# Layer one's last pair in seven partial second products, and block 2's low parts written in layer two

## The chip, the cores and the metric

One core of one Trainium2 chip runs the whole program. The metric is the device time of one execution in microseconds (us). Its engines are TensorE (PE in the rows; PEld is its weight loads), VectorE (DVE), ScalarE (ACT), GpSimd (POOL) and SyncE (SP), which issues the transfers. Each works through its own instructions in order and waits on semaphores of the others.

## The reference

Attention with cluster masks feeds two feed-forward layers, one after the other:

```
x = attention(q, k, v, centroids)             # 1536 tokens x 512, all float32
x = g1(x @ moe_w_in) @ moe_w_out              # 512 -> 2048 -> 512, g1(h) = max(0.01 h, h)
y = g2(x @ moe2_w_in) @ moe2_w_out            # 512 -> 2048 -> 512, g2(h) = relu(h) * relu(h)
```

## The kernel before, in words

The change lies in the two layers, so only these are told. Activations lie in SBUF transposed: features on the 128 partitions, tokens along the free axis. The 1536 tokens are three blocks of 512 (block 0, 1, 2), and the 512 features are four groups `o` of 128.

**Split products.** A float32 operand is kept as two parts in the format that TensorE multiplies: a high part (`xh`, `wh`, `gh`, `th`), which is the rounded value and is written by ScalarE, and a low part (`xl`, `wl`, `gl`, `tl`), which is the value minus its high part and is written by VectorE or GpSimd. A product is three matmuls: high by high, and each high by the other's low.

**Pairs.** A layer's 2048 inner features are 16 groups `f` of 128, worked on two at a time: a pair. First products make `h` (input weights by `x`) in the four banks U, V, W, X (`bank(i)`, tile `h`). Activations make `gh` and `gl`. Second products multiply these by the output weights into banks `o0` to `o3`, and `flush` adds them to the sums `acc` in SBUF, one 128x512 tile for each block and group.

**Seven for eight.** A pair with its two blocks 0 and 1 is a 2x2 product. In `quad` the first products are done with seven partial products in place of eight, on sums of weights (blocks with j = 2, made on GpSimd) and on sums of `x` (`th`, `tl`, made by `t_ops`). In `seven`, for the pairs listed in `SEVEN`, the second products are too: M1 to M7 on sums of the output weights (j = 3) and on sums of activations (T1 to T4). `rN.j` flushes partial product N. Block 2 is done plainly (`u0`, `u1`, then `o0` to `o3` with `f0` to `f3`).

**What sets the order.** In the layers the order on every engine but SP is the program's: the strings `SEVEN_QUAD` and the like are lists of steps that are issued one after the other, and the lists in `step_list` are interleaved with tables (`TURN`, `TURN_LAST`, `TURN_SEAM`, `SUMS`) that say after which step a piece of the coming weights or of the `x` sums is issued. The pieces of a weight block are: 0 load, 1 magnitude on ScalarE and `low` on GpSimd (L200), 2 join on VectorE (L206), 3 high part on ScalarE (L167), 4 low part on GpSimd (L168). One buffer `wraw` holds a load, so the next load starts when the join before it is done.

**The seam.** Pair 14 is layer one's last. There `flush` makes the new `x`: it adds, ScalarE writes `xh` and then `xl` is written, by GpSimd for blocks 0 and 1. For block 2 the sum stays in the bank (`o`), and VectorE subtracts from there, all four groups at the end. Pair 14 uses `quad` and plain second products (48 matmuls for blocks 0 and 1, `g2`). Layer two's first pair is plain: its steps are unit (0,0), unit (0,1), unit (1,0), out (0,0), unit (1,1), out (0,1), unit (2,0) and so on, 12 matmuls each, where unit (b,j) reads `xh` and `xl` of block b, all four groups in turn.

Of the kernel before, what the change touches and what calls it, by code (L numbers as in the profile page):

```python
# [80 lines left out]
def attention_moe_moe_kernel(  # L81
# [26 lines left out]
    SEVEN = (4, 6, 8, 10, 12)  # L108
# [53 lines left out]
    def split_block(ci, t):  # L162
        pool = next(q for q, n in ring if ci % RING < n)
        wh = pool.tile([128, 2 * DM], F32R, tag="wh", name="wh")
        wl = pool.tile([128, 2 * DM], F32R, tag="wl", name="wl")
        weights[blocks[ci]] = (wh, wl)
        nc.scalar.copy(out=wh, in_=t)  # L167
        return lambda: nc.gpsimd.tensor_tensor(  # L168
            out=wl, in0=t, in1=wh.bitcast(F32), op=ALU.subtract
        )  # L170

    def decode_pieces(ci):
# [41 lines left out]
        def rest():  # L214
            st["rest"]()
# [11 lines left out]
    def sum_pieces(ci):  # L227

        st = {}
        K = DM // 2  # L230

        def sums():
            w = st["w"] = stg[1].tile([128, 4, K], F32, tag="ws", name="ws")
            m, f, j = blocks[ci]
            t0, t1 = (words[blocks.index((m, f, i))] for i in range(2))
            if j == 2:
                a11, a12, a21, a22 = t0[:, 0:K], t0[:, K : 2 * K], t1[:, 0:K], t1[:, K : 2 * K]
            else:
                a11, a12, a21, a22 = (
                    t[:, DM + i * K : DM + (i + 1) * K] for i in range(2) for t in (t0, t1)  # L240
                )
            for o, i, k, op in (
                (w[:, 0], a21, a22, ALU.add),
                (w[:, 1], w[:, 0], a11, ALU.subtract),
                (w[:, 2], a11, a21, ALU.subtract),
                (w[:, 3], a12, w[:, 1], ALU.subtract),
            ):
                nc.gpsimd.tensor_tensor(out=o, in0=i, in1=k, op=op)

        def high():  # L250
            st["rest"] = split_block(ci, st["w"].rearrange("p a b -> p (a b)"))

        return [sums, high, lambda: st["rest"]()]
# [772 lines left out]
    x_low = []  # L1026

    def flush(m, b, g, o, ps, part=slice(0, 512)):
# [30 lines left out]
    def quad(m, f, behind=True):  # L1059
# [11 lines left out]
        def first():  # L1071
            p(U, lambda k: w_in(f0, k), lambda k: x_in(k, 0), True)
            p1 = tmp()
            nc.scalar.copy(out=p1, in_=U)
            p(V, lambda k: w_in(f0, 2 + k), lambda k: x_in(2 + k, 0), True)
            add(V, V, p1)
            if behind:
                act(m, 0, f, V)
# [3 lines left out]
        def second():  # L1082
# [4 lines left out]
            if not behind:  # L1087
                act(m, 0, f, V)
# [30 lines left out]
    def seven(f, prev, after, later):  # L1119
# [119 lines left out]
        for name, q, block, c, g, b, half in (  # L1239
# [8 lines left out]
            for j in range(2):  # L1248
                ops[f"r{name}.{j}"] = lambda q=q, j=j, b=b, o=2 * half + j: flush(
                    0, b, f // 2, o, st[q, j]  # L1250
# [8 lines left out]
        for o in range(4):  # L1259
            ops[f"o{o}"] = lambda o=o: last(o)  # L1260
            ops[f"f{o}"] = lambda o=o: flush(0, 2, f // 2, o, st["o", o])
        for i, q in enumerate(prev):
            ops[f"bh{i}"] = lambda q=q: g2(*q)
        for c, base in (("n", after), ("l", later), ("c", (0, f))):
            for k in range(4):
                for j in range(5):
                    ops[f"{c}{k}.{j}"] = lambda base=base, k=k, j=j: piece((*base, k), j)
        for kk in range(2):
            ops[f"h4.{kk}"] = t_by[0][kk]["h4"]
        for name in (SEVEN_PLAIN if f < 2 * PLAIN[0] else SEVEN_QUAD).split():  # L1270
# [66 lines left out]
    def step_list(m, f, prev):  # L1337
# [18 lines left out]
        first, second, third = quad(m, f, bool(behind))  # L1356
        behind = behind or [lambda: None] * 2
# [14 lines left out]
    TURN_LAST = TURN[:9] + (  # L1372
        TURN[9] + ((3, 1),), ((3, 2),), ((4, 0),), (),
    )
    TURN_SEAM = (
        (), ((0, 3),), ((1, 1),), ((0, 4), (1, 2)), (), ((2, 0), (3, 0)),
# [10 lines left out]
            -2: "t1.0 t1.1 t2.0 t2.1", -1: "t4.0 t4.1", 0: "t3.0 t3.1", 2: "h1.0 h1.1 l1.0 l1.1",  # L1387
# [6 lines left out]
    def piece(block, j):  # L1394
# [5 lines left out]
        pieces[block][j]()  # L1400
# [12 lines left out]
    for m in range(2):  # L1413
        turn = 0
        for f in range(0, NF, 2):
# [18 lines left out]
            for i, step in enumerate(seq):  # L1434
# [5 lines left out]
                table = {(0, NF - 2): TURN_LAST, (1, 0): TURN_SEAM}.get((m, f), TURN)  # L1440
# [5 lines left out]
                if m == 0 and f == NF - 2:  # L1446
                    sums(1, i - len(seq))
# [48 lines left out]
```

## Time and profile before

| | |
|---|---|
| time, median of 3 runs | 744.39 us (744.38 to 744.74) |
| the profiled execution's own time | 744.36 us |
| its span, first to last instruction | 742.6 us |
| TensorE busy | 735.8 us, 99% |
| VectorE, ScalarE, GpSimd busy | 533.1, 453.4, 494.1 us |
| layer one's pairs 6 to 12 | 30.00 us each |
| pair 14, then layer two | from 455.82 us, from 487.67 us |

Busy time is a union over an engine's instructions, and TensorE's overlap: a 512-column matmul lasts 0.39 us, and the next starts 0.23 us after it. The chain of waits counts each instruction from where the one before it ended. Lines L1 to L1495 are those of the kernel before.

### The profile page before, as it was taken

The page shows a single profiled execution, that of the slowest core. Times are in us where ns is not written, and L with a number is a line of the kernel's source. Part 1 is how long each engine was busy: PE and PEld are TensorE (multiplying, and loading weights), DVE is VectorE, ACT ScalarE, POOL GpSimd, SP SyncE. Part 2 cuts the span into 40 slices and gives each one's busy share as a digit, 9 for nine tenths or more (in the row PEclk, how much of TensorE's full clock was granted, in tenths as well). Part 3 has the DMA queues.
Part 4 walks back from the last instruction along what each step waited for, and adds up shares of the span by engine and source line. Part 5 has one row for each costly group of instructions (what it writes and reads, how often), then busy time and mean ns, then how long its engine had stood idle before and what let it go on. Part 6 is the DMA issues. An engine that isn't in the chain of part 4 may idle for free.

```text
span 742.6 us, 11189 instructions
## 1 busy us (share of the span) xinstructions
PE 735.8 (99%) x4018; PEld 641.2 (86%) x4018; DVE 533.1 (72%) x844; ACT 453.4 (61%) x837; POOL 494.1 (67%) x465
## 2 busy tenths in 40 slices
PE   9999999999999999999999999999999999999998
PEld 8999999999998878888888888888888888888886
DVE  7999999999997535477676866564666666676655
ACT  7988988988997564456365373656634335443430
POOL 7999999999957738686787883699434343343400
PEclk9999999999999999999999999999999999999999
DMA  5694574572603311112121131111312112121004
GB/s 148 167 222 113 117 181 109 107 189 67 164 1 116 113 57 57 56 57 99 59 71 56 57 114 47 67 58 56 101 42 85 57 57 77 45 106 58 1 0 170
DMA packets 16727, 65.52 MB, mean 88 GB/s; under 512 B 3120, under 2 KB 4272, under 8 KB 11680
## 3 DMA queue, kind: packets, MB, share of 16 engines
q1 hardware_dynamic: 16672, 64.81, 29.7%
q8 instruction: 32, 0.52, 0.3%
q14 instruction: 23, 0.19, 0.1%
HBM read 43.02 MB, written 3.15 MB: 62 GB/s over the span
## 4 chain that ended last, share of the span: by engine, by line
PE 93%; ACT 3%; DVE 2%; POOL 1%; issue 1%; POOLq 0%; ACTq 0%; DVEq 0%
PE h L914 32%; PE o L992 23%; PE A L578 8%; PE S L481 7%; PE T L543 7%; PE o L1221 6%; PE h L1221 4%; PE S L351 1%; ACT e L513 1%; DVE nm L503 1%; PE warm L291 1%; PE o L1022 1%; DVE el L560 1%; ACT eh L554 0%; PE dots L351 0%
## 5 line engine op out<-in xcount | busy, mean ns | idle before, releaser
L168 POOL TENSOR_TENSOR wl<-wt,wh 128x1024 fp32r<-128x1024 f32 x32 | 77.4, 2420 | 74.4 <-ACT wh L167 73.9
L914 PE MATMUL h<-xh,wh 128*128 128x512 f32 x288 | 112.1, 391 | 0.3 <-DVE h L1067 0.3
L914 PE MATMUL h<-xh,wl 128*128 128x512 f32 x288 | 112.2, 390 | 0.0
L914 PE MATMUL h<-xl,wh 128*128 128x512 f32 x288 | 112.1, 389 | 0.0
L1034 DVE TENSOR_TENSOR acc<-o,acc 128x512 f32<-128x512 f32 x154 | 100.0, 686 | 11.8 <-PE o L992 11.8
L560 DVE TENSOR_TENSOR el<-T,eh 128x512 fp32r<-128x512 f32 x144 | 94.6, 683 | 2.8 <-ACT eh L554 2.0
L530 POOL TENSOR_SCALAR e<-e,r 128x768 f32<-128x768 f32 x96 | 86.8, 917 | 12.5 <-PE T L543 6.7
L503 DVE TENSOR_REDUCE nm<-S 128x1 f32<-128x768 f32 x96 | 90.9, 949 | 3.6 <-PE S L351 1.9
L513 ACT ACTIVATE e<-S,nm 128x768 f32<-128x768 f32 x96 | 87.2, 909 | 9.9 <-DVE ds L379 5.4
L481 PE MATMUL S<-hb 128*128 128x384 f32 (+1 forms) x384 | 89.4, 347 | 0.4 <-ACT xt L591 0.3
L554 ACT CAST eh<-T 128x512 fp32r<-128x512 f32 x144 | 79.7, 590 | 8.8 <-PE T L543 8.6
L963 DVE TENSOR_TENSOR gl<-h,gh 128x512 fp32r<-128x512 f32 x66 | 45.0, 691 | 54.0 <-ACT h L958 35.5
L578 PE MATMUL A<-eh,vv 128*128 128x256 f32 x288 | 80.3, 308 | 0.6 <-DVE xt L600 0.6
L543 PE MATMUL T<-ident,e 128*128 128x128 f32 x576 | 79.7, 273 | 0.5 <-POOL e L530 0.5
L578 PE MATMUL A<-el,vv 128*128 128x256 f32 x288 | 73.0, 283 | 0.2 <-DVE el L560 0.2
L543 PEld LDWEIGHTS T<-ident,e 128*128 128x128 f32 x576 | 68.9, 143 | 3.6 <-POOL e L530 0.7
L992 PE MATMUL o<-wh,gh 128*128 128x512 f32 x184 | 71.6, 389 | 0.0
L992 PE MATMUL o<-wl,gh 128*128 128x512 f32 x184 | 71.6, 389 | 0.0
L992 PE MATMUL o<-wh,gl 128*128 128x512 f32 x184 | 71.6, 389 | 0.0
L948 ACT ACTIVATE t<-h 128x512 f32<-128x512 f32 x48 | 28.0, 599 | 71.3 <-PE h L914 38.0
L168 POOL TENSOR_TENSOR wl<-ws,wh 128x1024 fp32r<-128x1024 f32 x17 | 41.4, 2434 | 38.3 <-ACT wh L167 38.3
L914 PEld LDWEIGHTS h<-xh,wh 128*128 128x128 f32 x288 | 54.1, 188 | 12.5 <-DVE gl L1181 0.8
(187 smaller groups left out, 1739.9 us busy)
## 6 DMA issues: line engine op xcount, KB each, us to landing
wraw<-w SPq DMA_DIRECT2D x32, 1024.0 KB, 4.7
hb<-spl SPq DMA_DIRECT2D x14, 576.0 KB, 4.7
hb<-spl SPq DMA_DIRECT2D x42, 192.0 KB, 5.1
rqk<-qk SPq DMA_DIRECT2D x16, 384.0 KB, 4.0
rv<-v SPq DMA_DIRECT2D x8, 384.0 KB, 3.5
out<-q SPq DMA_DIRECT2D x11, 256.0 KB, 2.0
hb<-st SPq DMA_DIRECT2D x56, 24.0 KB, 2.1
hb<-hb SPq DMA_DIRECT2D x5, 144.0 KB, 8.2
```

Of the source, the lines that this page charges most:

```text
L168: return lambda: nc.gpsimd.tensor_tensor(out=wl, in0=t, in1=wh.bitcast(F32), op=ALU.subtract)
L481: nc.tensor.matmul(out=s[:, c, 0:HALF], lhsT=hb[0:k, a, i * 128 : (i + 1) * 128], rhs=hb[0:k, b, c * HALF : (c + 1) * HALF], start=(a == 0 ...
L503: nc.vector.tensor_reduce(out=n, in_=s_t[t][:, :, 0:HALF], axis=AX.XY, op=ALU.max, negate=True)
L513: nc.scalar.activation(out=e.rearrange("p (a b) -> p a b", a=2), in_=s_t.pop(t)[:, :, 0:HALF], func=AF.Exp, bias=n_t.pop(t), scale=1.0, ac ...
L530: nc.gpsimd.tensor_scalar(out=e_t[t], in0=e_t[t], scalar1=r_t[t // 2][:, t % 2 : t % 2 + 1], scalar2=1.0, op0=ALU.mult, op1=ALU.mult,)
L543: nc.tensor.transpose(T[:, o : o + 128], e_t[2 * u + b][:, kc * 128 : (kc + 1) * 128], ident)
L554: nc.scalar.copy(out=eh[:, 2 * g : 2 * g + 2, :].rearrange("p a b -> p (a b)"), in_=T_t[u, g])
L560: nc.vector.tensor_tensor(out=el[:, 2 * g : 2 * g + 2, :].rearrange("p a b -> p (a b)"), in0=T_t.pop((u, g)), in1=eh[:, 2 * g : 2 * g + 2, ...
L578: nc.tensor.matmul(out=A, lhsT=w, rhs=m[:, kc, :], start=(kc == 0 and i == 0), stop=(kc == KC - 1 and i == 1),)
L914: nc.tensor.matmul(out=out, lhsT=l, rhs=r, start=(first and i == 0), stop=(i == n - 1), skip_group_check=not first,)
L992: nc.tensor.matmul(out=outs[o], lhsT=l, rhs=r, start=(first and i == 0), stop=(last and i == 2),)
L1034: nc.vector.tensor_tensor(out=a, in0=ps, in1=a, op=ALU.add)
```

## The change

Pair 14 joins `SEVEN`, with an order of its own, `SEVEN_LAST`. Its first 54 products are in the order of the other pairs; the second products are M1 to M7 (42 matmuls) for blocks 0 and 1. A fourth weight block, (0, 14, 3), is made for it. The sum for `x` now ends in `acc` for every block, also for block 2, and its low part reads `acc` and `xh`, both in SBUF. For blocks 0 and 1 GpSimd writes it as before, but for block 0's groups 2 and 3 VectorE does (`x0.2`, `x0.3`), and for block 2 VectorE does so in layer two, two groups after step 3 and two after step 4 of its first pair. The `x` sums t1, t2 and t4 move into `SEVEN_LAST`, and of weight block (1, 2, 0) the join and of (1, 2, 1) the load move from pair 14 to step 0 of layer two.

```diff
+SEVEN_LAST = SEVEN_FIRST + (
+    "M1 M2 r1.0 r1.1 r2.0 r2.1 B22l l0.0 u1 u1h u1f u1l M6 M5 r6.0 r5.0 r5.1 r6.1 o0 f0 M3 T4h r3.0 M7 "
+    "r7.0 T4l r7.1 r3.1 o1 f1 M4 r4.0 r4.1 x0.2 x0.3 l0.1 t1.0 t1.1 t2.0 t2.1 t4.0 t4.1 o2 f2 o3 f3"
+)
...
-    SEVEN = (4, 6, 8, 10, 12)
+    SEVEN = (4, 6, 8, 10, 12, 14)
...
-    def flush(m, b, g, o, ps, part=slice(0, 512)):
+    def flush(m, b, g, o, ps, part=slice(0, 512), later=None):
...
-            x, eng = (ps, nc.vector) if b == 2 else (a, nc.gpsimd)
-            nc.vector.tensor_tensor(out=x, in0=ps, in1=a, op=ALU.add)
-            nc.scalar.copy(out=xh[:, o, c], in_=x)
-            if b == 2:
-                x_low.append((o, c, x))
-                if o < 3:
-                    return
...
+            nc.vector.tensor_tensor(out=a, in0=ps, in1=a, op=ALU.add)
+            nc.scalar.copy(out=xh[:, o, c], in_=a)
+
+            def low(eng):
+                eng.tensor_tensor(
+                    out=xl[:, o, c], in0=a, in1=xh[:, o, c].bitcast(F32), op=ALU.subtract
+                )
+
+            if later is not None:
+                later[b, o] = low
             else:
...
+                low(nc.gpsimd)
...
+            ops[f"f{o}"] = lambda o=o: flush(0, 2, f // 2, o, st["o", o], later=x_low)
+            ops[f"x0.{o}"] = lambda o=o: x_low[0, o](nc.vector)
...
-            return seq + [lambda: g2(*tail[0]), lambda: g2(*tail[1])], []
...
     TURN_SEAM = (
-        (), ((0, 3),), ((1, 1),), ((0, 4), (1, 2)), (), ((2, 0), (3, 0)),
+        ((0, 2), (1, 0)), ((0, 3),), (), ((1, 1), (0, 4)), ((1, 2),), ((2, 0), (3, 0)),
...
-            -2: "t1.0 t1.1 t2.0 t2.1", -1: "t4.0 t4.1", 0: "t3.0 t3.1", 2: "h1.0 h1.1 l1.0 l1.1",
+            0: "t3.0 t3.1", 2: "h1.0 h1.1 l1.0 l1.1",
...
+                if (m, f) == (1, 0) and i in (3, 4):
+                    for o in (2 * i - 6, 2 * i - 5):
+                        x_low[2, o](nc.vector)
```

VectorE, at the seam, before: the first three rows close layer one (the third is block 2's low parts, read from the banks `o`), the others are the activations of layer two's first units and the join of `wt`.

```order
L206 SCALAR_TENSOR_TENSOR wt<-wt,wraw 128x1024
L1039 TENSOR_TENSOR o<-o,acc 128x512 x4
L1050 TENSOR_TENSOR xl<-o,xh 128x512 x4
L951 SCALAR_TENSOR_TENSOR h<-h,t 128x512
L963 TENSOR_TENSOR gl<-h,gh 128x512
L951 SCALAR_TENSOR_TENSOR h<-h,t 128x512
L963 TENSOR_TENSOR gl<-h,gh 128x512
L951 SCALAR_TENSOR_TENSOR h<-h,t 128x512
L963 TENSOR_TENSOR gl<-h,gh 128x512
L206 SCALAR_TENSOR_TENSOR wt<-wt,wraw 128x1024
```

VectorE, the same place, after, from the low parts of block 0's groups 2 and 3 to the last two of block 2.

```order
L1045 TENSOR_TENSOR xl<-acc,xh 128x512 x2
L1041 TENSOR_TENSOR acc<-h,acc 128x512 x2
L956 SCALAR_TENSOR_TENSOR h<-h,t 128x512
L968 TENSOR_TENSOR gl<-h,gh 128x512
L211 SCALAR_TENSOR_TENSOR wt<-wt,wraw 128x1024
...
L968 TENSOR_TENSOR gl<-h,gh 128x512
L1045 TENSOR_TENSOR xl<-acc,xh 128x512 x2
L956 SCALAR_TENSOR_TENSOR h<-h,t 128x512
L968 TENSOR_TENSOR gl<-h,gh 128x512
L211 SCALAR_TENSOR_TENSOR wt<-wt,wraw 128x1024
L1045 TENSOR_TENSOR xl<-acc,xh 128x512 x2
```

The four low parts of block 2 stand in two twos now, the second behind the activations of unit (1,1) and behind the join of weight block (1, 2, 1).

GpSimd at the seam, before: low parts of `x` (L1050), sums of `x` (L1289) and their low parts (L1295), and weights (L200 and L168).

```order
L1050 TENSOR_TENSOR xl<-acc,xh 128x512 x4
L168 TENSOR_TENSOR wl<-wt,wh 128x1024
L200 TENSOR_SCALAR wraw<-wraw 128x1024
L1050 TENSOR_TENSOR xl<-acc,xh 128x512 x4
L1289 TENSOR_TENSOR q<-acc 128x512 x2
L1289 TENSOR_TENSOR q<-acc,q 128x512 x2
L1289 TENSOR_TENSOR t_5861<-acc,q 128x512
L1289 TENSOR_TENSOR t_5863<-acc,q 128x512
L1289 TENSOR_TENSOR q<-acc 128x512 x2
L200 TENSOR_SCALAR wraw<-wraw 128x1024
L1295 TENSOR_TENSOR tl<-q,th 128x512 x2
L168 TENSOR_TENSOR wl<-wt,wh 128x1024
```

GpSimd, the same place, after.

```order
L173 TENSOR_TENSOR wl<-wt,wh 128x1024
L1045 TENSOR_TENSOR xl<-acc,xh 128x512 x6
L205 TENSOR_SCALAR wraw<-wraw 128x1024
L1297 TENSOR_TENSOR q<-acc 128x512 x2
L1297 TENSOR_TENSOR q<-acc,q 128x512 x2
L1297 TENSOR_TENSOR t_5862<-acc,q 128x512
L1297 TENSOR_TENSOR t_5864<-acc,q 128x512
L1297 TENSOR_TENSOR q<-acc 128x512 x2
L1303 TENSOR_TENSOR tl<-q,th 128x512 x2
L205 TENSOR_SCALAR wraw<-wraw 128x1024
L173 TENSOR_TENSOR wl<-wt,wh 128x1024
L1303 TENSOR_TENSOR tl<-q,th 128x512 x2
```

Two low parts of `x` fewer, and the second `wraw` step (L205), for which VectorE's second join waits, stands behind two `tl` instead of ahead of them; a `wl` of 1024 columns follows it at once.

## Rows read from the trace of the kernel before

**Rows 1.** The page: each engine's busy time, then the granted clock by slice.

```profile
PE 735.8 (99%) x4018; PEld 641.2 (86%) x4018; DVE 533.1 (72%) x844; ACT 453.4 (61%) x837; POOL 494.1 (67%) x465
PEclk9999999999999999999999999999999999999999
```

**Rows 2.** Waits of TensorE: who was waited for: us in total, times, longest.

```profile
PE h L914 <- DVE h L1067: 0.3, 1, 0.3
```

**Rows 3.** Chain of waits, pairs 12 and 14: start, us, engine, tile, line, count.

```profile
425.82 12.24 PE h L914 x54
...
440.78 2.80 PE h L914 x12
...
446.30 1.36 PE h L1221 x6
...
455.82 5.46 PE h L914 x24
...
487.67 8.16 PE h L914 x36
```

**Rows 4.** Timeline of TensorE in pair 14: start, us, instruction, idle before it.

```profile
455.66 0.39 PE L914 MATMUL h<-xh,wh 128*128 128x512 f32 x1
...
463.59 0.39 PE L914 MATMUL h<-xh,wl 128*128 128x512 f32 x1
464.26 0.50 PE L914 MATMUL h<-xh,wh 128*128 128x512 f32 x1 [0.28 <-DVE h L1067]
464.60 0.40 PE L914 MATMUL h<-xl,wh 128*128 128x512 f32 x1
```

**Rows 5.** Timeline of VectorE at the seam.

```profile
483.29 1.23 DVE L206 SCALAR_TENSOR_TENSOR wt<-wt,wraw 128x1024 int32<-128x1024 int32 x1 [0.33 <-POOL wraw L200]
...
488.32 2.48 DVE L1050 TENSOR_TENSOR xl<-o,xh 128x512 fp32r<-128x512 f32 x4
```

**Rows 6.** Timeline of GpSimd at the seam.

```profile
489.38 2.55 POOL L1289 TENSOR_TENSOR q<-acc 128x512 f32<-128x512 f32 x2
...
499.54 1.12 POOL L200 TENSOR_SCALAR wraw<-wraw 128x1024 int32<-128x1024 uint32 x1
500.74 3.58 POOL L1295 TENSOR_TENSOR tl<-q,th 128x512 fp32r<-128x512 f32 x2
504.27 2.41 POOL L168 TENSOR_TENSOR wl<-wt,wh 128x1024 fp32r<-128x1024 f32 x1
```

**Rows 7.** Timeline in layer two's second pair, VectorE's rows, with two SBUF inputs.

```profile
515.71 1.81 DVE L1333 TENSOR_TENSOR xl<-t,xh 128x512 fp32r<-128x512 f32 x1 [0.77 <-ACT xh L1332]
518.17 2.16 DVE L1333 TENSOR_TENSOR xl<-t,xh 128x512 fp32r<-128x512 f32 x1 [0.65 <-ACT xh L1332]
```

**Rows 8.** The same stretch, GpSimd's rows.

```profile
514.56 2.41 POOL L168 TENSOR_TENSOR wl<-wt,wh 128x1024 fp32r<-128x1024 f32 x1
516.91 2.87 POOL L168 TENSOR_TENSOR wl<-ws,wh 128x1024 fp32r<-128x1024 f32 x1
```

**Rows 9.** Timeline early in layer one: a join, then a two-input VectorE subtraction, and GpSimd.

```profile
282.88 1.23 DVE L206 SCALAR_TENSOR_TENSOR wt<-wt,wraw 128x1024 int32<-128x1024 int32 x1 [0.91 <-POOL wraw L200]
284.03 1.78 DVE L1283 TENSOR_TENSOR q<-xh,xl 128x512 f32<-128x512 f32 x1
...
282.93 2.33 POOL L1295 TENSOR_TENSOR tl<-q,th 128x512 fp32r<-128x512 f32 x1
```

**Rows 10.** Timeline at the seam: the activation of layer two's first unit.

```profile
490.43 0.60 ACT L948 ACTIVATE t<-h 128x512 f32<-128x512 f32 x1 [1.40 <-PE h L914]
...
492.41 0.69 DVE L963 TENSOR_TENSOR gl<-h,gh 128x512 fp32r<-128x512 f32 x1 [0.65 <-ACT gh L960]
```

**Rows 11.** Issues of transfers at the seam: the load of a weight block, KB, us to landing.

```profile
wraw<-w SPq DMA_DIRECT2D x1, 1024.0 KB, 4.8
```

**Rows 12.** Timeline of GpSimd around the border of pairs 12 and 14.

```profile
451.81 1.12 POOL L200 TENSOR_SCALAR wraw<-wraw 128x1024 int32<-128x1024 uint32 x1
463.92 2.40 POOL L168 TENSOR_TENSOR wl<-wt,wh 128x1024 fp32r<-128x1024 f32 x1 [10.99 <-ACT wh L167]
```

More of the change, by code (lines that the diff above doesn't have):

```diff
@@ L251, in high @@
             st["rest"] = split_block(ci, st["w"].rearrange("p a b -> p (a b)"))
-        return [sums, high, lambda: st["rest"]()]
+        return [sums, high, lambda *eng: st["rest"](*eng)]
     def pool_copy(out, in_):
@@ L1057, in flush, with quad @@
             nc.sync.dma_start(out=out[r : r + 128, part], in_=ob)
-    def quad(m, f, behind=True):
+    x_low = {}
+    def quad(m, f):
         f0, f1, s = ((m, f, j) for j in range(3))
@@ L1076, in first @@
             add(V, V, p1)
-            if behind:
-                act(m, 0, f, V)
+            act(m, 0, f, V)
         kept = []
@@ L1086, in second @@
                 nc.scalar.copy(out=kept[-1], in_=q)
-            if not behind:
-                act(m, 0, f, V)
         def third():
@@ L1215, in seven @@
             ops[n + "l"] = lambda n=n, eng=eng: low(n, eng)
+            ops[n + "lD"] = lambda n=n: low(n, nc.vector)
         def second(out, ws, g, fresh, stop=True):
@@ L1248, in seven @@
             for j in range(2):
-                ops[f"r{name}.{j}"] = lambda q=q, j=j, b=b, o=2 * half + j: flush(
-                    0, b, f // 2, o, st[q, j]
+                g = f // 2 if f < NF - 2 or name in "2347" else 1
+                ops[f"r{name}.{j}"] = lambda q=q, j=j, b=b, g=g, o=2 * half + j: flush(
+                    0, b, g, o, st[q, j], later=x_low if b == 0 and o > 1 else None
                 )
@@ L1267, in seven @@
                     ops[f"{c}{k}.{j}"] = lambda base=base, k=k, j=j: piece((*base, k), j)
+                    ops[f"{c}{k}.{j}D"] = lambda base=base, k=k, j=j: piece(
+                        (*base, k), j, nc.vector
+                    )
         for kk in range(2):
             ops[f"h4.{kk}"] = t_by[0][kk]["h4"]
-        for name in (SEVEN_PLAIN if f < 2 * PLAIN[0] else SEVEN_QUAD).split():
+            for name in ("t1", "t2", "t4"):
+                ops[f"{name}.{kk}"] = t_by[1][kk][name]
+        order = SEVEN_PLAIN if f < 2 * PLAIN[0] else SEVEN_QUAD if f < NF - 2 else SEVEN_LAST
+        for name in order.split():
             ops[name]()
@@ L1354, in step_list @@
             return seq, tail
-        first, second, third = quad(m, f, bool(behind))
-        behind = behind or [lambda: None] * 2
+        first, second, third = quad(m, f)
         seq = [
@@ L1392, in attention_moe_moe_kernel, with piece @@
     pieces = {}
-    def piece(block, j):
+    def piece(block, j, *eng):
         if block not in blocks:
@@ L1399, in piece @@
             pieces[block] = (sum_pieces if block[2] > 1 else decode_pieces)(i)
-        pieces[block][j]()
+        pieces[block][j](*eng)
     def pair_after(m, f):
@@ L1439, in attention_moe_moe_kernel @@
                     piece((0, 2, 0), 0)
-                table = {(0, NF - 2): TURN_LAST, (1, 0): TURN_SEAM}.get((m, f), TURN)
+                table = TURN if (m, f) != (1, 0) else TURN_SEAM
                 for k, j in table[i] if i < len(table) else ():
```

28 lines of the change are left out of this document (7 added, 21 removed), and 4 rows, old and new, of the table SUMS.

## The prediction

> **What bounds the kernel now.** First the page: TensorE is busy 99% of the span and its granted clock is full in every slice [rows 1]. Then TensorE's waits: in the two layers only one of note, 0.28 us on VectorE [rows 2, 4]. So the chain of waits through the layers is a row of matmuls without a hole: 12 of 512 columns take 2.72 us, 0.227 us each, and a seven-product pair takes 30.00 us from one start to the next (455.82 - 425.82) [rows 3]. Then the timelines of VectorE and GpSimd at the seam, because a change there counts only if it shortens TensorE's row or makes it wait: VectorE has holes, GpSimd has almost none from 489 to 507 us [rows 5, 6].
>
> **What it removes.** Pair 14 has 138 matmuls now (42 + 24 first products, 48 + 24 second) and 132 after it (42 for 48). Six by 0.227 is -1.36 us. The pair's one wait goes with `quad`'s order: from 463.59 to 464.60 us two starts take 1.01 us where 0.45 would do, -0.56 us [rows 4]. The seven-product order has a small one of its own at `u1`, 2.80 for 2.72 [rows 3], +0.08 us. Together -1.84 us, and by the chain: 31.85 us from pair 14 to layer two (487.67 - 455.82) become 30.00 [rows 3], -1.85. If nothing else happened, 744.36 - 1.85 = 742.5 us; the profiled execution (744.36) stands 0.03 below the median, so the sums need no other correction.
>
> **What it adds and hides.** The fourth weight block costs GpSimd four short sums and a `wl` of 2.4 us, and ScalarE a high part. The other seven-product pairs do the same within 30.00 us, and GpSimd is idle for 10.99 us just there [rows 12]: 0. The last sums of pair 14 are followed by six to twelve matmuls of `o2`, `o3` and by layer two's first six, over 4 us, and the chain add, high part, low part is 0.7 + 0.6 + 0.6 [rows 10]: 0, but see the port below. Were it bare, that chain would cost its 1.9 us once.
>
> **The low parts of block 2.** This is where the change decides. Before, VectorE's four low parts read a bank and SBUF, and take 0.62 us each with GpSimd at work all along [rows 5, 6]. After it they read `acc` and `xh`, two SBUF inputs. The nearest rows with two SBUF inputs, 128x512, are the `xl<-t,xh`: 1.81 and 2.16 us. The first starts at 515.71, GpSimd's `wl` ends at 516.97, and 0.55 us later the subtraction is done (517.52); the second ends at 520.33, 0.55 us after the next `wl` (519.78). GpSimd's next instruction in turn took 2.87 us for 2.41 [rows 7, 8]. So the two exclude each other for whole instructions. In [rows 9] a join holds GpSimd's `tl` back (2.33 us for 1.30), and the subtraction behind the join on VectorE then waits until that `tl` ends (285.26) and ends at 285.81: whoever waited first is next.
>
> The price of one low part is thus between 0.6 us (as the bank rows) and 0.55 us behind one whole GpSimd instruction: 1.30 for a `tl`, 2.41 for a `wl`. I take the second, since the form of [rows 7] is the same.
>
> By the row of the old low parts, 0.62 us each, the sum would be about 742.9 (the second rival). The Trainium skill says in "SBUF — State Buffer", section "Who interferes with whom", that a VectorE instruction with two SBUF inputs and a GpSimd instruction that reads SBUF block each other fully, and that one with at most one SBUF input does not; by it the sum is the 747.8 that follows. The trace agrees with both halves: 0.62 us with one SBUF input, 1.81 and 2.16 with two.
>
> **The clock of the seam, step by step.** TensorE: pair 14's first product starts at 455.66 [rows 4], so layer two's first is at 485.66 and unit (2,0), the seventh step of 2.72 us, at 501.98. In it group 2's low part is wanted by the eighth product, at 501.98 + 7 x 0.227 = 503.57, and group 3's by the eleventh, at 504.25.
>
> GpSimd: M7 of pair 14 ends at about 480.4 (after M1, M2, u1, M6, M5, o0, M3 in steps of [rows 3]). Its flushes and their high parts follow at 0.6 us each, so the last four of GpSimd's six low parts of `x` run from 480.2 at 1.25 each to 485.2. VectorE's `x0.2` is ready at 484.1, waits until 485.2 and is done at 485.75; the `wraw` step (1.11) lies between, and `x0.3` is done at 487.4. Layer two's first unit wants them at 487.25 and 487.93: in time, the second by 0.5 us. Then eight sums of `x` (10.1 us, [rows 6] give 2.55 for two) and one turn for VectorE's first join (1.1): 498.6. Then by turns low part 0 (0.55), `tl` (1.25), low part 1 (0.55), `tl` (1.25): 502.2. Then the `wraw` step (0.1 + 1.11): 503.35.
>
> VectorE's second join waits for that; its own queue is free at about 503.0 (unit (1,1) ends at 499.4, and `t`, `gh` and `gl` end some 2.7 us after a unit [rows 10], here a microsecond later since ScalarE first waits for the load: the first join ends at 493.5, landing takes 4.8 [rows 11], the magnitude 1.1). The join takes 1.23: 504.6. In this time GpSimd's `wl` of 1024 columns has come to wait, as the `tl` in [rows 9], so it goes next: 506.95. Then low part 2: 507.5. Then GpSimd's next `tl`, 1.25, and low part 3: 509.3.
>
> TensorE so waits at the eighth product from 503.57 to 507.55, 3.98 us, and at the eleventh from 508.23 to 509.35, 1.12 us. Behind the waiting matmul stands all of TensorE's queue, so both are lost whole. After a wait the first start is 0.11 us late (464.26 to 464.60 is 0.34, [rows 4]): 0.22 for two. Sum: 744.36 - 1.85 + 3.98 + 1.12 + 0.22 = 747.8 us.
>
> What is late later: the second pair's summed weights, the `wl` that ends at 519.78 now [rows 8]. By the same steps it ends at about 521, and TensorE comes to it 3.4 us later than now (-1.85 + 5.1 + 0.2): 0.
>
> Bounds: if no low part waits for the port, 742.9; if GpSimd's two instructions are as long as its long rows (2.87 and 1.31) and the load lands 0.4 later, about 1 us on top, 748.9.
>
> **Rivals.**
>
> *The last two low parts go straight after the join, ahead of the `wl`.* Both are ready when the join ends. For it: VectorE's queue is contiguous. Against: [rows 9], where GpSimd got the turn. They would be done at 505.15 and 505.75, TensorE loses about 1.7 us with the restart: 744.2, no change.
>
> *No port wait (the other side: faster).* From 0.6 us a low part GpSimd's line is shorter and the join is set by `gl` of unit (1,1), at about 502.1; join 503.3, group 2's low part 503.9, a wait of 0.35: 744.36 - 1.85 + 0.35 = 742.9. For it: [rows 5]. Against: [rows 7, 9]. It decides from the point where the turns saved exceed 3.3 us.
>
> *The waiting costs clock too.* The longest wait of TensorE in the layers is 0.28 us now and its clock stays at 2.4 GHz [rows 1, 2]; no row shows it after a wait of 4 us. If the clock fell to 1.2 GHz for one group of 12 matmuls, these would take 2.72 us more: 750.5. The Trainium skill, "TensorE: Matmul & The Clock Gate", section "HAM oscillation — how this bites in real kernels", says that idle gaps send the array back to half its clock; no run here shows it.
>
> *Pair 14 or the seam is not as smooth as the other pairs*, say `x0.3` late by 0.5 us: it only adds to the forecast and lies in its range.
>
> **How the numbers follow.** Forecast, both low parts behind the port, 746.9 to 748.9: 0.76. Straight after the join, 743.5 to 745.5: 0.06. No port wait: 0.11, and since 742.9 lies at the edge of what can be told from no change (0.2%, 1.5 us: 742.9 and 745.9), I split it, 0.08 faster and 0.03 same. Lower clock: 0.07. So faster 0.08, same 0.09, slower 0.83. The range must leave out no more than 2 in 10: from 745.6, which leaves out the two rivals below, to 750.6, which takes in the lower clock.
>
> **What would show it.** Right: pair 14 lasts 30.0 us with 132 matmuls and layer two starts at 485.8; in TensorE's waits stands `h` on VectorE's `xl` with about 4 and 1.1 us, at 503.6 and 508.2; VectorE's third pair of `xl<-acc,xh` takes about 3.0 and 1.9 us, and the `wl` beside the second join some 3.5. Wrong: these rows at 0.7 us and no hole in unit (2,0), then the time is near 742.9; or a hole before 500 us, then I misjudged `x0.3` or a sum of pair 14.

## The result and the profile after

The changed kernel takes 748.82 us (748.03 to 750.70, 6 runs) where the kernel before takes 744.36: a ratio of 1.0065, interval 1.0051 to 1.008. (A ratio here is worked out over all runs of both kernels; the quotient of the two medians alone is 1.0060.) It is slower by 4.5 us; 747.8 had been forecast. The profiled execution took 748.16 us, its span is 746.3.

The change has one more part, which the account of it ahead and its diff leave out: in layer one's first pairs ScalarE's rounding of the first `x` sum (`h1.0` in `SUMS`) is issued one step later, and `l1.0` and `h2.0` with it. Its diff stands at e8.

The page of the changed kernel, TensorE's busy time and the granted clock by slice, against [rows 1], and under it the one new line in TensorE's waits, against [rows 2]:

```profile
PE 735.8 (99%) x4012; PEld 640.7 (86%) x4012; DVE 546.5 (73%) x855; ACT 455.7 (61%) x841; POOL 504.6 (68%) x472
PEclk9999999999999999999999999999999999999999
```

```profile
PE h L919 <- DVE xl L1045: 4.4, 1, 4.4
```

Six matmuls fewer, and yet the same 735.8 us busy: this is the first hint that some matmuls became slower, which the 40 slices (18.7 us each) of the clock are too coarse to show. The wait at `h` of [rows 2, 4] is gone from pair 14, and one of 4.4 us on VectorE's `xl` has come.

The chain of waits, against [rows 3] (start, us, what):

```profile
424.94 12.24 PE h L919 x54
...
454.91 12.24 PE h L919 x54
...
502.01 3.43 DVE wt L211
505.44 3.36 DVE xl L1045 x2
...
508.85 1.22 PE h L919 x2
510.07 3.08 PE o L997 x12
```

Pair 12 to pair 14 is 29.97 us. Inside unit (2,0) the chain leaves TensorE for VectorE's second join and its last two low parts, and behind them two matmuls take 1.22 us and twelve 3.08 where 0.45 and 2.72 are the rule. TensorE's timeline shows the same (against [rows 4]):

```profile
454.75 0.39 PE L919 MATMUL h<-xh,wh 128*128 128x512 f32 x1
...
484.71 0.39 PE L919 MATMUL h<-xh,wh 128*128 128x512 f32 x1
...
502.39 0.39 PE L919 MATMUL h<-xh,wh 128*128 128x512 f32 x1
507.16 0.74 PE L919 MATMUL h<-xl,wh 128*128 128x512 f32 x1 [4.38 <-DVE xl L1045]
507.69 0.63 PE L919 MATMUL h<-xh,wl 128*128 128x512 f32 x1
508.12 0.63 PE L919 MATMUL h<-xh,wh 128*128 128x512 f32 x1
508.85 0.80 PE L919 MATMUL h<-xl,wh 128*128 128x512 f32 x1
...
512.99 0.39 PE L919 MATMUL h<-xh,wh 128*128 128x512 f32 x1
```

Pair 14 takes 29.96 us (484.71 - 454.75). The eighth product of unit (2,0) starts 4.77 us after the seventh, and the next ones follow every 0.43 us and more, not every 0.227. The windows of the changed kernel (busy us and count of PE, PEld, DVE, ACT, POOL, then the granted clock) say why:

```profile
502.00:507.00 5.00, 0.78 (x4) 0.32 (x2) 5.00 (x3) 1.84 (x4) 5.00 (x3) 1.00 0.11 16
507.00:508.00 1.00, 0.84 (x2) 0.75 (x3) 1.00 (x2) 0.00 (x0) 1.00 (x1) 0.63 0.81 279
508.00:510.00 2.00, 1.91 (x5) 0.99 (x5) 0.79 (x1) 0.00 (x0) 1.92 (x3) 0.50 0.82 344
510.00:512.00 2.00, 2.00 (x9) 1.61 (x8) 0.70 (x1) 1.07 (x2) 2.00 (x4) 0.83 0.00 0
```

From 502 to 507 us TensorE is busy for 0.78 us, while VectorE and GpSimd show busy for the whole 5.00; then TensorE runs at 1.2 GHz for some 3 us.

VectorE's and GpSimd's timelines at the seam, against [rows 5] and [rows 6, 12]:

```profile
502.01 3.43 DVE L211 SCALAR_TENSOR_TENSOR wt<-wt,wraw 128x1024 int32<-128x1024 int32 x1
505.37 3.42 DVE L1045 TENSOR_TENSOR xl<-acc,xh 128x512 fp32r<-128x512 f32 x2
```

```profile
462.10 2.39 POOL L173 TENSOR_TENSOR wl<-wt,wh 128x1024 fp32r<-128x1024 f32 x1
...
500.80 1.12 POOL L205 TENSOR_SCALAR wraw<-wraw 128x1024 int32<-128x1024 uint32 x1
501.99 2.37 POOL L173 TENSOR_TENSOR wl<-wt,wh 128x1024 fp32r<-128x1024 f32 x1
504.31 3.92 POOL L1303 TENSOR_TENSOR tl<-q,th 128x512 fp32r<-128x512 f32 x2
```

The join that takes 1.23 us alone takes 3.43: it ends 1.08 us after the `wl`. The two low parts behind it take 3.42 us, and two `tl` 3.92, not 2.55. A busy row here is for the most part a wait.

One more difference lies in a place the prediction did not speak of, where the later rounding acts. In layer one's first pairs, TensorE in the kernel before:

```profile
260.40 1.20 PE L992 MATMUL o<-gh,wh 128*128 128x512 f32 x4 [0.17 <-ACT gh L957]
261.62 0.50 PE L992 MATMUL o<-gl,wh 128*128 128x512 f32 x1
```

and in the changed one:

```profile
259.84 1.07 PE L997 MATMUL o<-gh,wh 128*128 128x512 f32 x4
260.79 0.50 PE L997 MATMUL o<-gl,wh 128*128 128x512 f32 x1
```

With ScalarE's rounding of the first x sum one unit later, `gh` is there in time.

Two lengths carry the comparison: pair 14, and layer two from its first product to the end of the span. Both are read from TensorE's timeline and the span of each profile.

| kernel | median us | pair 14 | layer two |
|---|---|---|---|
| before | 744.36 | 31.85 | 255.1 |
| changed | 748.82 | 29.96 | 261.6 |
| changed again | 749.71 | 29.96 | 263.0 |
| e3: lows read a bank | 745.18 | 29.97 | 257.8 |
| e4: lows ahead of join | 746.44 | 30.00 | 260.2 |
| e1: lows two steps earlier | 746.17 | 30.00 | 259.5 |
| e2: `wl` two steps later | 749.53 | 30.00 | 260.0 |
| e6: 18 matmuls in the wait | 747.67 | 29.96 | 259.7 |
| e10: e6 and e2 | 747.61 | 29.99 | 260.8 |
| e5: lows alone | 749.42 | 31.85 | 260.6 |
| e8: rounding alone | 743.88 | 31.85 | 255.1 |
| x4: all lows in layer one | 742.12 | 29.97 | 255.4 |
| e9: x4, rounding back | 742.79 | 29.99 | 255.5 |

The changed kernel's span thus is -0.9 ahead of pair 14 (455.66 - 454.75), -1.9 in it, +6.5 in layer two: +3.7 us.

### The profile page after: what moved, and what is told of

The parts are those of the page before. It is cut to its first block, busy times and chain, and to the rows that moved or that the text cites. A ratio compares the mean times of both kernels' runs of the same rounds, so it can differ in the third digit from the quotient of the medians.

```text
span 746.3 us, 11210 instructions
## 1 busy us (share of the span) xinstructions
PE 735.8 (99%) x4012; PEld 640.7 (86%) x4012; DVE 546.5 (73%) x855; ACT 455.7 (61%) x841; POOL 504.6 (68%) x472
## 4 chain that ended last, share of the span: by engine, by line
PE 90%; DVE 4%; ACT 4%; issue 1%; POOL 1%; POOLq 0%; ACTq 0%; DVEq 0%
PE h L919 31%; PE o L997 20%; PE A L583 8%; PE S L486 7%; PE o L1221 7%; PE T L548 7%; PE h L1221 4%; PE S L356 1%; ACT e L518 1%; DVE xl L1045 1%; DVE nm L508 1%; DVE wt L211 1%; PE warm L296 1%; PE o L1027 1%; DVE el L565 1%
## 5 line engine op out<-in xcount | busy, mean ns | idle before, releaser
L1037 DVE TENSOR_TENSOR acc<-o,acc 128x512 f32<-128x512 f32 x160 | 103.7, 685 | 11.8 <-PE o L997 11.8
L968 DVE TENSOR_TENSOR gl<-h,gh 128x512 fp32r<-128x512 f32 x60 | 40.9, 691 | 44.6 <-ACT h L963 24.5
L173 POOL TENSOR_TENSOR wl<-ws,wh 128x1024 fp32r<-128x1024 f32 x18 | 43.3, 2407 | 42.8 <-ACT wh L172 42.8
L919 PEld LDWEIGHTS h<-xl,wh 128*128 128x128 f32 x288 | 54.2, 188 | 16.5 <-DVE xl L1045 5.6
```

Source lines behind the costliest of these rows:

```text
L173: return lambda eng=nc.gpsimd: eng.tensor_tensor(out=wl, in0=t, in1=wh.bitcast(F32), op=ALU.subtract)
L919: nc.tensor.matmul(out=out, lhsT=l, rhs=r, start=(first and i == 0), stop=(i == n - 1), skip_group_check=not first,)
L1037: nc.vector.tensor_tensor(out=a, in0=ps, in1=a, op=ALU.add)
```

## The experiments

The theories, which are not exclusive: 1, VectorE's instructions with two SBUF inputs take turns with whole GpSimd instructions; 2, the low parts are late only by their place in VectorE's queue; 3, TensorE's wait costs it clock as well; 4, the later rounding is worth something of its own. The kernel before stood at 744.23, 744.00 and 744.47 us in the three sets of runs (e3, e4, e6, x4; then e2, e1, e5 and the repetition; then e8 to e10). Every run also has a granted clock, the mean over its span, which tells that the clock fell somewhere in it but not where. In the kernel before it is 1.000 in 55 of these 56 runs; in the changed kernel's twelve (first measurement and repetition) it is never: 0.998 in five (747.88 to 748.66 us), 0.995 in six (748.97 to 750.70) and 0.991 in one (752.37).

**e3: one SBUF input instead of two.**

```
-                        x_low[2, o](nc.vector)
+                        nc.vector.tensor_tensor(
+                            out=xl[:, o, c], in0=banks_of[1, 1, i - 3],
+                            in1=xh[:, o, c].bitcast(F32), op=ALU.subtract,
+                        )
```

> The changed kernel, but block 2's four low parts in layer two take a PSUM bank as their first operand in place of `acc`, so they have one SBUF input; place, size and queue are the same. This leaves out block 2's right low parts: the bank holds other numbers. Theory 1 (turns with GpSimd for two SBUF inputs): the low parts take 0.7 us each, GpSimd's `tl` between them are no longer held back, and of the two waits in unit (2,0) the second goes. The first stays in part, since the second weight join still has two SBUF inputs and still waits for the `wl`: about 3 us from the join's end at 505.4, so the time is about 2 us below the changed kernel's, 746 to 747 us. Theory 2 (the low parts are late only by their place in VectorE's queue): nothing changes, 748 to 749 us. Theory 3 (the clock): if a wait of 3 us is enough for the granted clock to fall, the two groups of matmuls behind it run at below 1.0, 0.5 to 1 us more.

745.18 us, ratio 1.0019 (1.0004 to 1.0034). VectorE's timeline, then GpSimd's, then TensorE's:

```profile
502.21 2.53 DVE L211 SCALAR_TENSOR_TENSOR wt<-wt,wraw 128x1024 int32<-128x1024 int32 x1
504.66 1.28 DVE L1456 TENSOR_TENSOR xl<-h,xh 128x512 fp32r<-128x512 f32 x2
```

```profile
501.26 2.39 POOL L173 TENSOR_TENSOR wl<-wt,wh 128x1024 fp32r<-128x1024 f32 x1
```

```profile
505.39 0.50 PE L919 MATMUL h<-xl,wh 128*128 128x512 f32 x1 [2.43 <-DVE xl L1456]
```

Same place, same size, same queue: two low parts take 1.28 us and not 3.42. Theory 2 falls. The join still ends 1.09 us after the `wl`. I expected 3 us of wait and got 2.43, since the first two `tl` too were no longer held back and the `wraw` step came earlier. The clock stayed at 1.00 in this profile, and its mean is 1.000 in six of the ten runs (744.24 to 745.44 us); in the other four (745.92 to 750.52) it is 0.993 to 0.998. The Trainium skill, "SBUF — State Buffer", section "Who interferes with whom", makes the same distinction between one and two SBUF inputs on VectorE; this pair of runs agrees with it on both sides.

**e4: the low parts ahead of the join.**

```
+                if (m, f) == (1, 0) and i in (3, 4):
+                    for o in (2 * i - 6, 2 * i - 5):
+                        x_low[2, o](nc.vector)
                 table = TURN if (m, f) != (1, 0) else TURN_SEAM
...
                 sums(m, turn)
-                if (m, f) == (1, 0) and i in (3, 4):
-                    for o in (2 * i - 6, 2 * i - 5):
-                        x_low[2, o](nc.vector)
```

> The changed kernel, but in steps 3 and 4 of layer two the low parts are issued ahead of the step's weight pieces, so that low parts 2 and 3 stand before the second join and not behind it. Theory 1 (turns): the low parts no longer pay for the join's wait for the `wl`, but each still waits for one GpSimd instruction: waits of about 0.5 and 2.2 us in unit (2,0) in place of 4.4 and 0.5, the time about 2 us below the changed kernel's, 746 to 747 us. Theory 2 (only the place in the queue behind the join): all four are done before TensorE wants them, no wait, and the time is that of the shorter pair 14, 742.5 us. Theory 3 (the clock): with no wait above 2.3 us the granted clock stays at 1.00, or falls if this is already enough.

746.44 us, ratio 1.0033 (1.0019 to 1.0047). VectorE's timeline and TensorE's two waits:

```profile
502.07 4.31 DVE L1045 TENSOR_TENSOR xl<-acc,xh 128x512 fp32r<-128x512 f32 x2
```

```profile
504.75 0.50 PE L919 MATMUL h<-xl,wh 128*128 128x512 f32 x1 [2.16 <-DVE xl L1045]
...
506.44 0.69 PE L919 MATMUL h<-xl,wh 128*128 128x512 f32 x1 [0.71 <-DVE xl L1045]
```

First in VectorE's queue, they still wait: 2.16 and 0.71 us. The expected two waits came in the other order, because the `wl` had begun at 501.79 and the first low part waited for it to end. After the second wait the clock was 0.50 from 507 to 510 us in this profile; of the seven runs, three have a mean of 1.000 (745.51 to 745.68 us) and the others 0.993 to 0.998.

**e6: TensorE kept busy during the wait.**

```
+                if (m, f, i) == (1, 0, 6):
+                    spare = bank(0)
+                    for n in range(18):
+                        nc.tensor.matmul(
+                            out=spare, lhsT=weights[1, 0, 0][0][:, 0:128], rhs=xh[:, 0, 0:N],
+                            start=True, stop=True,
+                        )
```

> The changed kernel with 18 more matmuls of 512 columns between out(0,1) and unit (2,0) of layer two, into a spare bank; their result is discarded. They take 18 x 0.227 = 4.1 us of the time in which TensorE now waits for low part 2. Theory 3 (the wait costs clock): the granted clock stays at 1.00 from 500 to 515 us, unit (2,0) waits about 0.3 us for low part 2 and 1.0 us for low part 3, and though TensorE does 4.1 us more work the time falls by what the low clock costs in the profiled run, (1.22 - 0.45) + (3.08 - 2.72) = 1.1 us: about 747.1, and runs at 749 to 751 us no longer occur. If the clock falls for another reason than the wait: rows at below 1.0 stay, and the time is 748 to 751 us. If GpSimd's and VectorE's chain does not set the end of the wait: the added matmuls come on top, about 752 us.

747.67 us (746.30 to 748.28), ratio 1.0045 (1.0033 to 1.0058): with 4.1 us more work it is 1.1 us faster than the changed kernel, the size expected from the rows, and no run came above 748.3. In its profile the clock is 1.00 from 500 to 515 us, and its mean is 1.000 in all five runs, as in all five of e10, where it is below that in all twelve of the changed kernel. With the wait filled the clock does not fall: it is the wait that takes it down. How much of the 1.1 us is the clock is less clear, for the profile holds a surprise, first GpSimd's row, then VectorE's:

```profile
502.11 3.48 POOL L173 TENSOR_TENSOR wl<-wt,wh 128x1024 fp32r<-128x1024 f32 x1
```

```profile
502.12 1.22 DVE L211 SCALAR_TENSOR_TENSOR wt<-wt,wraw 128x1024 int32<-128x1024 int32 x1
503.25 2.89 DVE L1045 TENSOR_TENSOR xl<-acc,xh 128x512 fp32r<-128x512 f32 x1
```

Here `wl` and join come 0.01 us apart and the join goes first, as the prediction had it; in the changed kernel's profile they came 0.02 us apart and the `wl` went first. Low part 2 is done at 506.14 us here (503.25 + 2.89), and there TensorE could start behind it at 507.16: the order of the turns is worth 1 us. In this profile, then, unit (2,0) gains from the order as well as from the clock, and it is the fastest of the five runs (746.30; the others take 747.55 to 748.28). Which order those had is not known.

**The changed kernel again**, to see the order and the clock once more.

> The changed kernel once more, unchanged. In its first profile GpSimd's `wl` and VectorE's second join came to the port 0.02 us apart, and `wl` got the turn; in the run with 18 added matmuls the join did. Theory 1 (turns, decided by hundredths of a microsecond): if the join goes first this time, low part 2 is done 1.0 us earlier (about 506.1 us against 507.11) and the first wait is about 3.4 us; else 4.4 us as before. Theory 3 (clock): the granted clock falls behind the wait in either case, and the times spread over 747 to 751 us. Median 748 to 749.5 us.

749.71 us (747.88 to 752.37), ratio 1.0077 (1.0062 to 1.0092). The `wl` went first again (504.92, the join 505.10), and the wait was again 4.4 us. The profiled run was the longest, 752.37: it was 2.9 us late before pair 12 already, and behind the wait the clock stayed down longer (windows as above):

```profile
510.00:512.00 2.00, 1.88 (x4) 1.07 (x5) 1.71 (x2) 0.00 (x0) 2.00 (x2) 0.50 0.96 377
512.00:514.00 2.00, 2.00 (x5) 1.58 (x6) 0.29 (x1) 0.60 (x1) 1.92 (x4) 0.50 0.24 98
514.00:516.00 2.00, 2.00 (x6) 1.55 (x5) 1.10 (x2) 1.56 (x3) 1.73 (x2) 0.50 0.00 0
```

The same wait, 1.4 us more in layer two (263.0 against 261.6).

**e2: the `wl` out of the way.** In `TURN_SEAM`:

```
-        ((0, 2), (1, 0)), ((0, 3),), (), ((1, 1), (0, 4)), ((1, 2),), ((2, 0), (3, 0)),
+        ((0, 2), (1, 0)), ((0, 3),), (), ((1, 1),), ((1, 2),), ((0, 4), (2, 0), (3, 0)),
```

> The changed kernel, but GpSimd's `wl` of the block whose join stands before low part 2 is issued two steps later, behind both `tl`. Theory 1 (turns with GpSimd): the 2.37 us instruction leaves the turns, a `tl` of 1.25 takes its place, so low part 2 is 1.1 us earlier or, if a `tl` gets the turn ahead of the join, 0.5 to 1 us earlier: waits of 2.9 to 3.9 us and up to 1.1 us in unit (2,0), the time 0.5 to 1.5 us below the changed kernel's, 747 to 748 us. Theory 2 (only the place in VectorE's queue): the join, and low part 2 behind it, come as before; no change, 748 to 750 us. Theory 3 (clock): unless the wait gets clearly shorter, the granted clock falls again.

The profile is as theory 1 has it: the join takes 1.22 us from 502.21, the waits are 2.19 and 0.73 us, and that run took 746.69 us. But the median is 749.53 (4 runs), ratio 1.0068 (1.0053 to 1.0082), no better than the changed kernel. The time is a miss. The profiled run has a mean clock of 0.998 and lies 1.2 to 2.0 us below the five of the changed kernel that have the same; the other three (749.39 to 750.40) have 0.995, as the changed kernel's six between 748.97 and 750.70. An estimate from these two figures: a mean that is lower by 0.003 over 749 us is 2.2 us lost against the full clock, about as far as the two groups are apart. e10 was run to settle it.

**e10: e2 and the 18 matmuls together,** by the two diffs above.

> The 18 added matmuls (result discarded) together with the `wl` issued two steps later. Without the added matmuls the later `wl` shortened the first wait in its profile to 2.2 us, but the median did not fall, with the granted clock at 0.50 behind the wait. Theories 1 and 3 together: with TensorE kept busy the clock stays at 1.00, low parts 2 and 3 are done by 505.1 and 506.8 us as in that profile, before TensorE comes to them at 506.8 and 507.5 us, so no wait is left: the median is 0.3 to 1.3 us below the 747.67 of the 18 matmuls alone, 746.3 to 747.3 us. If the clock was not what hid the gain: no difference, 747.7 us.

747.61 us, ratio 1.0042 (1.0028 to 1.0055), no gain over e6. GpSimd's timeline, then VectorE's:

```profile
502.63 3.53 POOL L1303 TENSOR_TENSOR tl<-q,th 128x512 fp32r<-128x512 f32 x2
506.12 2.82 POOL L173 TENSOR_TENSOR wl<-wt,wh 128x1024 fp32r<-128x1024 f32 x1
```

```profile
502.88 2.13 DVE L211 SCALAR_TENSOR_TENSOR wt<-wt,wraw 128x1024 int32<-128x1024 int32 x1
504.94 4.56 DVE L1045 TENSOR_TENSOR xl<-acc,xh 128x512 fp32r<-128x512 f32 x2
```

With the clock at 1.00, low part 2 is on time, but in this execution a `tl` took the turn ahead of the join and so the `wl` the one ahead of low part 3, which is done at 509.50 (504.94 + 4.56); TensorE waits 1.36 us there. So with the clock at 1.00, which its mean shows for all five runs, moving the `wl` gains nothing over e6, and in the profile the reason is the order of the turns: a long instruction put two steps later only meets the next victim. Which one is decided by little: the `tl` starts 0.25 us ahead of the join here (502.63 and 502.88), and in e2's profile the join starts 0.01 us ahead of the `tl` (502.21 and 502.22). This does not settle what e2's three slower runs lost: a lower clock is on record for them, their order of turns is not.

**e1: the low parts two steps earlier.**

```
-                if (m, f) == (1, 0) and i in (3, 4):
-                    for o in (2 * i - 6, 2 * i - 5):
+                if (m, f) == (1, 0) and i in (1, 2):
+                    for o in (2 * i - 2, 2 * i - 1):
```

> The changed kernel, but the four low parts of block 2 are issued behind steps 1 and 2 of layer two instead of steps 3 and 4, while GpSimd does the sums of x. Theory 1 (turns): they are long done when unit (2,0) wants them, but each pays for one GpSimd instruction all the same, and holds back both VectorE's queue and GpSimd's: no wait in unit (2,0), about 0.9 us in out(1,0) for `gh`, and 2 to 3 us in the next pair for the summed weights' `wl` (around 519 us). Time about 1.7 us over the kernel before, 745.5 to 746.5 us. Theory 2 (place in the queue): no wait anywhere, 742.5 us. Theory 3 (clock): the granted clock stays at 1.00 through unit (2,0).

746.17 us, ratio 1.0034 (1.002 to 1.0047). Unit (2,0) has no wait. Out(1,0) waits 0.25 us, less than the 0.9 expected, and by the profile for ScalarE's copy `acc<-o` and not for `gh`. GpSimd's timeline, and TensorE's, in the second pair, and the windows behind it:

```profile
518.16 2.80 POOL L173 TENSOR_TENSOR wl<-ws,wh 128x1024 fp32r<-128x1024 f32 x1
```

```profile
521.01 0.50 PE L919 MATMUL h<-th,wl 128*128 128x512 f32 x1 [1.87 <-POOL wl L173]
```

```profile
522.00:524.00 2.00, 2.00 (x7) 1.53 (x7) 1.28 (x2) 0.87 (x2) 0.18 (x1) 0.60 0.00 0
524.00:526.00 2.00, 2.00 (x7) 1.59 (x6) 0.00 (x0) 0.78 (x2) 0.00 (x0) 0.55 0.54 143
```

The turns that VectorE takes are lost to GpSimd, and come due 15 us later, at the place expected. The clock is 1.00 through unit (2,0), as theory 3 has it, but falls to 0.60 and 0.55 behind this wait of 1.87 us.

**e5: the low parts alone.** The kernel before, with block 2's sum in `acc` and its low parts on VectorE in layer two's steps 3 and 4; pair 14 in its old order.

```
-            x, eng = (ps, nc.vector) if b == 2 else (a, nc.gpsimd)
+            x, eng = a, nc.gpsimd
...
+                if (m, f) == (1, 0) and i in (3, 4):
+                    for o in (2 * i - 6, 2 * i - 5):
+                        x_low[o]()
```

> The kernel before (its pair 14 of quad order kept), with one thing of the change: block 2's sum goes to `acc`, and its four low parts (two SBUF inputs) are issued by VectorE in layer two, two each in steps 3 and 4. Theory 1 (turns): unit (2,0) waits about 0.7, 2.2 and 1.1 us, so the time is 744.3 + 4.1 = 748.4 us, 747.5 to 749 with the order of the turns, more if the clock falls. The change is then worth -1.85 us for pair 14 and about +5 us for the low parts. Theory 2 (place in the queue): the low parts take 0.7 us each and come in time, 744.3 us.

749.42 us, ratio 1.0071 (1.0058 to 1.0084). TensorE's timeline:

```profile
510.47 0.50 PE L914 MATMUL h<-xl,wh 128*128 128x512 f32 x1 [0.46 <-DVE xl L1042]
...
513.25 0.50 PE L914 MATMUL h<-xl,wh 128*128 128x512 f32 x1 [1.81 <-DVE xl L1042]
...
514.94 0.50 PE L914 MATMUL h<-xl,wh 128*128 128x512 f32 x1 [0.71 <-DVE xl L1042]
```

Three waits at the expected places; layer two is 5.5 us longer than before, the clock (0.50 from 516 to 519 us) included. Its profiled run (754.94) was 5 us late by pair 12 already, so only pair 14 and layer two are read from it.

**e8: the rounding alone.**

```
-            7: "w12.0 w11.0", 8: "t1.0 w22.0", 9: "t2.0 h1.0", 10: "l1.0 h2.0",
-            11: "t3.0 w21.0", 12: "l2.0 h3.0", 13: "t4.0", 14: "l3.0",
+            7: "w12.0 w11.0", 8: "t1.0 w22.0", 9: "t2.0", 10: "h1.0",
+            11: "l1.0 h2.0 t3.0 w21.0", 12: "l2.0 h3.0", 13: "t4.0", 14: "l3.0",
```

> The kernel before with only the third part of the change: ScalarE's rounding of the first sum of x one unit later in layer one's first pairs. In the traces so far TensorE starts the four matmuls behind the 24 low-part products at 260.40 us before and at 259.84 us after the change, and ScalarE's rounding (`th<-q`, 258.72 us) stands ahead of the `gh` that they wait for. Theory 4 (this part is worth something of its own): the wait of 0.17 us on `gh` goes with the slow starts behind it, 0.5 to 0.6 us, so the first product of pair 12 comes at about 425.1 us instead of 425.66, and the time is 743.4 to 743.8 us. Rival (the 0.9 us by which the changed kernel was early is a difference between executions): the wait stays or comes back elsewhere, 744.0 to 744.4 us.

743.88 us against 744.47, ratio 0.9990 (0.9981 to 1.0000): -0.6 us, at the edge of what the runs can tell, and the wait on `gh` is gone from the profile. The profiled run, the fastest of the eleven, reaches pair 14 at 454.29 us, 1.4 us before the kernel before does: more than this part was expected to give.

**x4: all low parts with one SBUF input.** Block 2's sums stay in their banks and their low parts are issued in layer one; `x0.2` and `x0.3` read their bank too.

```
-    ... M4 r4.0 r4.1 x0.2 x0.3 l0.1 ... o2 f2 o3 f3"
+    ... M4 r4.0 r4.1 x2.1 x0.2 x0.3 l0.1 ... o2 f2 o3 x2.2 f3 x2.3"
...
-            nc.vector.tensor_tensor(out=a, in0=ps, in1=a, op=ALU.add)
-            nc.scalar.copy(out=xh[:, o, c], in_=a)
+            x = ps if b == 2 or later is not None else a
+            nc.vector.tensor_tensor(out=x, in0=ps, in1=a, op=ALU.add)
+            nc.scalar.copy(out=xh[:, o, c], in_=x)
+            if b == 0 and later is not None:
+                nc.scalar.copy(out=a, in_=x)
```

> Pair 14 as in the changed kernel, but all low parts on VectorE have one SBUF input: block 2's sums of x stay in their banks and the four low parts are issued in layer one behind their sums (banks 3, 2, 1, 3 for o0 to o3), and x0.2 and x0.3 read their bank too (ScalarE copies that sum to `acc`). No low part is left in layer two. Theory 1 (turns): GpSimd waits for VectorE's joins alone, no wait in unit (2,0), pair 14 stays at 30.0 us, so the time is 744.36 - 1.85 plus 0 to 0.7 for a small wait at a bank in layer two's second unit: 742.5 to 743.2 us. Theory 2 (place in the queue): the same. If the banks held longer by the low parts are what decides: a wait of 1 to 2 us in units (0,0) or (0,1) of layer two, 743.5 to 744.5 us.

742.12 us, ratio 0.9977 (0.9967 to 0.9988): faster than both kernels, by more than was expected. Pair 14 is 29.97 us, layer two 255.4. This run changes two things at once, the inputs of the low parts and their place; e3 is the one that changes the inputs alone. VectorE's second join still waits for GpSimd, but nothing urgent stands behind it:

```profile
503.97 2.29 DVE L211 SCALAR_TENSOR_TENSOR wt<-wt,wraw 128x1024 int32<-128x1024 int32 x1
506.33 0.70 DVE L956 SCALAR_TENSOR_TENSOR h<-h,t 128x512 f32<-128x512 f32 x1
```

**e9: x4 with the rounding back in its old place.**

> The kernel with all low parts in layer one (all on one SBUF input), but with the rounding of the first sum of x in its old place. Theory 4: the 0.17 us wait on `gh` at 260 us comes back with its slow starts, +0.5 to 0.6 us over the 742.12 measured, 742.6 to 742.8 us. Rival (difference between executions): 742.1 us, no such wait.

742.79 us, ratio 0.9981 (0.9972 to 0.9990); the wait of 0.16 us on `gh` is back. The two ratios differ by 0.04%, less than their intervals; the medians and the rows go the way of theory 4, which so stays likely and not shown.

## Why the prediction was right, and where not

- *Pair 14, -1.85 us.* Right: 29.96 us, with its own wait gone; e5 and e8, which keep the old order, have 31.85.
- *What was costed at nothing.* Right: no hole before 500 us, the fourth block's `wl` (462.10, 2.39 us) and the second pair's `wl` hide. e1 shows that the latter had little room.
- *The price of a low part, behind a whole GpSimd instruction.* Right, and shown by e3 (0.68 us each with one input) and e4, e5.
- *The first wait, 3.98 us and 0.11 of restart.* Measured 4.54 (507.16 - 502.39 - 0.227). Two steps behind it were off and partly cancel: relative to TensorE, GpSimd's `wraw` step ended 0.5 us earlier than I had worked out (501.92, against 503.35 with everything 0.95 us earlier, 502.40), and the turn I gave to the join went to the `wl`, so a `tl` came in between: 1 us more. e6 had the order of the prediction. So of the rows named as signs the wait of about 4 us came, but the `wl` took 2.37 us and not 3.5, the join 3.43, and the two low parts 3.42 together and not 4.9. (A slip besides: 502.2 and 1.21 make 503.41, not 503.35.)
- *The second wait, 1.12 us and 0.11.* At full clock the eleventh product would have stood at 507.16 + 0.34 + 2 x 0.227 = 507.95; it started at 508.85: 0.9 us, and 0.1 for the restart behind the first wait. In TensorE's waits it does not stand, since the slow matmul ahead of it lasts until 508.75 (508.12 + 0.63).
- *The clock, a rival with a chance of 0.07.* It did come, on top of the forecast's mechanism. From start to start, the fourteen matmuls from 508.85 to 512.99 us take 4.14 us where 14 x 0.227 = 3.18 is the rule: 1.0 us in the first profile, 0.1 of it restart. (The chain's rows give (1.22 - 0.45) + (3.08 - 2.72) = 1.1, since they count a slow matmul to its end.) The prediction had put 2.7 us on it, for one group of 12, and a chance of 0.07; that I held it for unlikely is its main fault. With the 0.9 us, 747.8 would have become 748.7. The Trainium skill, "TensorE: Matmul & The Clock Gate", section "HAM oscillation — how this bites in real kernels", warns of idle gaps; the trace agrees, with 0.50 from 508 to 510 us behind 4.4 us of waiting.
- *The later rounding.* The prediction has no term for it. Its wait of 0.17 us stood in TensorE's timeline before; e8 puts it at -0.6 us, at the edge of what the runs can tell.

So with its rounded terms layer two is 4.54 + 0.1 + 0.9 + 1.0 = 6.5 us longer, where 5.32 was forecast, and of the 0.9 us gained ahead of pair 14 the rounding may account for 0.6. The rest is not explained here; executions of the same stretch differ by as much (pair 14 starts at 454.29 us in e8's profile, at 454.75 in the changed kernel's and at 455.37 in e10's, all with the later rounding). That is the account of the profiled execution, 748.16 us. The median is 0.7 us higher, since three of the six runs have a mean clock of 0.995 where that one has 0.998. That the forecast came within 1 us of the median is thus in part luck: the clock and the turn of the `wl`, which it left out, were for the most part made up by the earlier `wraw` step and the 0.9 us ahead of pair 14. The rival without a port wait falls with e3 (0.68 us is the price with one SBUF input only), the one with both low parts straight behind the join with the 3.42 us that the two take.

## What to carry to other kernels

Before an elementwise operation is moved on VectorE, count its SBUF inputs: reading one operand from a PSUM bank kept the same subtraction at 0.68 us, and from SBUF it took a whole instruction of GpSimd more. Moving such an operation, or the GpSimd instruction beside it, only chose where the turn was paid (e1, e2, e4, e10); taking the second SBUF input away took the price of the low parts away (e3, where the join ahead of them kept its own), and with the low parts moved into layer one as well the change paid (x4). Where TensorE is the bound, price a wait of some microseconds, here 1.9 to 4.4, with the clock behind it, and look through the small waits of the profile for those that a change touches.

## What the runs showed of the hardware that was not expected

The order of two instructions whose recorded starts lie 0.01 to 0.02 us apart went either way, at 1 us a time (`wl` first in the changed kernel, the join first in e6 and e2). A wait of 2.43 us left the clock at 1.00 in e3's profile, while one of 1.87 us took it to 0.60 and below in e1's, and 2.16 and 0.71 us with 1.0 us of work between them to 0.50 in e4's, as did 2.19 and 0.73 in e2's. The length of the wait does not decide it alone: by their mean clocks, six of ten runs of e3 and three of seven of e4 kept the full clock, the others not. Behind the same wait of 4.4 us it stayed at 0.50 for some 3 us in one execution of the changed kernel and beyond 6 in another, and the two groups of that kernel's runs, 0.998 and 0.995, lie about 2 us apart. What sets this was not tried.
